# Attention beside a gated dense block on one core: three exponential patterns of a score tile, two of them summed by accumulating transfers

## The chip, the core and the metric

The kernel runs on one core of a Trainium2 chip. A core has a matrix engine (TensorE, PE in the profile), a vector engine (VectorE, DVE), a scalar engine (ScalarE, ACT), GpSimd (POOL) and SyncE (SP), which share an on-chip memory (SBUF). TensorE writes to a small accumulator memory (PSUM) that VectorE and ScalarE read. Transfers (DMAs) are issued from an engine's queue and run beside the engines; semaphores order all of it. The metric is the time of one execution on the device, in microseconds (us).

## The reference

The input `x` has 2048 rows of 512. All is bfloat16 at the ends.

```python
xn = _layernorm(x, axis=-1)
# A: 32 query heads of 16 on one shared key and value head
q = (xn @ wq) in 32 heads of 16;  k = xn @ wk;  v = xn @ wv
scores = einsum("bhqd,bkd->bhqk", q, k) * 16 ** -0.5
o = softmax(scores) @ v
s = o in one row of 512 @ wo
# B: dense 512 -> 1792 -> 512
g = silu(silu(xn @ w1) @ w2)
return x + s * g
```

## The kernel before, in words

**Tiles.** The queries are cut into four chunks of 512 and the heads into eight groups of four, so there are 32 groups of chunk and heads. A group has 16 key tiles of 128. A *tile* is a pair of group and key tile and has four *blocks*, one for each head: 128 keys by 512 queries. That makes 2048 blocks. A score matmul uses 32 rows of TensorE's array, so the four heads lie beside each other ("row" mode); the matmuls of the probabilities with V, and all dense ones, use 32 columns each, and four run beside each other ("col" mode). The planner calls four such a slot and gives a change of mode a price of its own.

**Two ways of taking an exponential.** A block goes to ScalarE or to VectorE.

- ScalarE (`exp_A`, line 576): TensorE puts two blocks into one of two PSUM pairs (`psA`, `fill_A`), and one instruction over 1024 columns writes both to `pa_sb`, a ring of 11. Each block is then owed one matmul with V (`emit_PV`, line 698).
- VectorE (`exp_D`, line 614): TensorE puts a block into one of three banks, `D`, `D1` or `F` (`fill_D`). VectorE adds a bias and writes the number as a 16-bit integer, whose bits read as bfloat16 are a piecewise linear power of two: a *pattern*. When the four blocks of a tile are there, GpSimd adds a constant to the integers (`shift`, line 639, as 64-bit words) and does so twice, which gives a second and a third pattern, shifted in phase. All three go into the sum with V, each with a weight of its own, so V is held four times (`vaug_sb`: once for ScalarE's blocks and once for each pattern). Such a tile is owed three matmuls with V for each block. A tile's patterns are held in one of four places (`ph_sb` three, `x_sb` one).

The last column of V's tile is the weight itself, so the same matmuls give the softmax's sum. When all that a group is owed has been added in `psO`, VectorE transposes it (`gn1`, line 769), takes the reciprocal (`gn2`), multiplies (`gn3`, line 786) and, for two groups, transposes back (`gn4`).

**Dense work.** The jobs `q` (queries), `h` (the first dense layer, 14 tiles of 512 for each chunk, into `u_sb`, two sets of 14), `z` (the second dense layer), `w` and `wp` (the product with `wo`) run on TensorE in bank `F`, between the scores (line 338). An `h` or a `z` is followed by a tanh on ScalarE (line 1014), 72 in all, and by a VectorE step (line 1046). A finished `w` goes through line 1058 into `fin_sb`, then an addition (line 1025) into `ob_sb`, and from there to the output.

**The order.** The queues of all engines are written out when the kernel is built. A class (`Sched`) holds a cost model of each engine and gives every instruction a due time; a loop emits, again and again, work for TensorE in col mode as long as ScalarE's next burst is not yet due, then a burst of scores for ScalarE (`score_run`) with blocks for VectorE riding in the rows that are free (`fill_D`); VectorE's steps are chosen by `advance_v`. A plan that does not come true on the chip is not mended there: each engine follows its written order and waits on semaphores.

Of the kernel before, what the change touches and what calls it, by code (L numbers as in the profile page):

```python
# [22 lines left out]
PH_SHIFT = (0, 43, 85)  # L23
PH_W = (0.2265625, 0.1787109375, 0.1416015625)
PH_ONE = 127 * 128
PH_BIAS = 65
NPH = len(PH_SHIFT)
LN2 = 0.6931471805599453
# [7 lines left out]
class Sched:  # L36
# [5 lines left out]
    def __init__(self):  # L42
        self.queues = {}
        self.done = {}
        self.clock = {}
        self.snap = {}
        self.last_w = {}
        self.readers = {}
        self.flagged = {}
        self.lanes = {}  # L50
        self.at = {}
        self.free = dict(pe=1.2, a=1.7, v=0.85, gp=0.7, sp=0.7)
        self.act_end = 0.0
        self.act_ends = []
        self.pe_mode, self.pe_last, self.pe_len, self.pe_tiles = None, 1.0, 0.0, set()
        self.pe_runs = []

# [37 lines left out]
    def model(self, eng, lane, cost, r):  # L95
        if lane:
# [27 lines left out]
        self.free[eng] = t + (cost or 0.4)  # L124
        return self.free[eng] + self.SEM
# [71 lines left out]
def bass_recurrent_scan__grouped_kv_mqa__dense_activation_silu__prompt_kernel(  # L197
# [25 lines left out]
    NPD = 4  # L223
    NPS = 3
    NGN = 2
    NOB = 4
    NWARM = 15
    NWARM2 = 0
    NWARM3 = 2
    NFRONT = 12  # L230
# [6 lines left out]
    NPAIR, LEAD_PAIR = 1, 1  # L237
    NF, F_FROM, F_LEFT, F_LATE, DENSE_END, HOLD, F_BEHIND = 14, 0.05, 9, 3, 0.97, 10, 0

    with ExitStack() as es:  # L240
# [15 lines left out]
        vaug_sb = sb("vaug_sb", [P, 1 + NPH, NKT, 32])  # L256
        qT_sb = sb("qT_sb", [P, 2, NDC, NQ])
        pa_sb = sb("pa_sb", [P, NPA, 2 * NQ])
        ph_sb = [sb(f"ph{j}_sb", [P, NPS, 4 * NQ], I16) for j in range(NPH)]
# [3 lines left out]
        u_sb = sb("u_sb", [P, 2, NFT, NQ])  # L263
        t_sb = sb("t_sb", [P, 2, NQ])
        tmp_sb = sb("tmp_sb", [P, 2, 4, D])
        fin_sb = sb("fin_sb", [P, 2, D])
# [6 lines left out]
        eps_sb = sb("eps_sb", [P, 1], FP32)  # L273
        mhalf_sb = sb("mhalf_sb", [P, 4], FP32)
        phw_sb = sb("phw_sb", [P, 1 + NPH], FP32)
# [37 lines left out]
        for j in range(NPH + 1):  # L313
            w = 1.0 if j == 0 else PH_W[j - 1]
# [40 lines left out]

        def aggr(t):
            op("v", lambda e: e.bn_aggr(mv_sb[:, t, :], stats_sb[:, t, :]), reads=[("st", t)], writes=[("mv", t)], cost=0.155)

        def rstd_pow(c):
            sl = slice(4 * c, 4 * c + 4)  # L360
            op("gp", lambda e: e.tensor_scalar(rstd_sb[:, sl], mv_sb[:, sl, 1], LN_EPS, None, op0=ALU.add),
               reads=[("mv", t) for t in tiles(c)], writes=[("rstd", c)])
            op("gp", lambda e: e.tensor_tensor(rstd_sb[:, sl], rstd_sb[:, sl], mhalf_sb[:, :], ALU.pow),  # L363
               reads=[("rstd", c), "mhalf"], writes=[("rstd", c)])
# [83 lines left out]
        def evac_V(c, bank, key):  # L448
            sh = [P, 1 + NPH, 4, DH]
# [26 lines left out]
        for t in tiles(0):  # L476
            stats(t)
        for t in tiles(0):
            aggr(t)
# [121 lines left out]
        def ph_ap(j, sl, a, b):  # L601
            if sl < 3:
                return ph_sb[j][:, sl, a:b]
            return x_sb[:, 4 * j:4 * j + 4, :].rearrange("p a b -> p (a b)").bitcast(I16)[:, a:b]

        def ph_key(j, sl, p):
            return ("ph", j, sl, p) if sl < 3 else ("x", 4 * j + p)

        def exp_D(blks):
# [8 lines left out]
            for b in blks:  # L618
                p = b["pos"]
                owe(tile[0], b["i"], tile[1], 1, ph_ap(0, sl, 512 * p, 512 * p + 512).bitcast(BF16), ph_key(0, sl, p), K.at[d])  # L620
# [8 lines left out]
        shifts = []  # L629

        def shift(tile, idx):
            sl, n = slot_of[idx], len(rows_of[idx])
            for j in range(1, NPH):
                if n < 4:
                    d = op("v", lambda e, j=j: e.tensor_scalar(ph_ap(j, sl, 0, NQ * n), ph_ap(0, sl, 0, NQ * n), float(PH_SHIFT[j]), None,
                                                               op0=ALU.add),
                           reads=[ph_key(0, sl, p) for p in range(n)], writes=[ph_key(j, sl, p) for p in range(n)], cost=0.4)
                else:
                    d = op("gp", lambda e, j=j: e.int64_add(ph_ap(j, sl, 0, 4 * NQ).bitcast(I64), ph_ap(0, sl, 0, 4 * NQ).bitcast(I64),  # L639
                                                            PH_SHIFT[j] * 0x0001000100010001),  # L640
                           reads=[ph_key(0, sl, p) for p in range(4)], writes=[ph_key(j, sl, p) for p in range(4)], cost=1.03)
                for p, i in rows_of[idx].items():
                    owe(tile[0], i, tile[1], 1 + j, ph_ap(j, sl, 512 * p, 512 * p + 512).bitcast(BF16), ph_key(j, sl, p), K.at[d])

        def may_D(blks):
            sl = slot_of[blks[0]["idx"]]
            return not any(held(ph_key(j, sl, p)) for j in range(1, NPH) for p in range(4)) and \
                not any(held(ph_key(0, sl, b["pos"])) for b in blks)
# [8 lines left out]
        def emit_PV(t, cap):  # L657
# [7 lines left out]
            while n < cap:  # L665
                cand = sorted((p for p in pend[gi] if p["at"] <= t + 0.216 * n and vready(p["kt"] // 4, t)), key=lambda p: p["at"])
# [28 lines left out]
                def f(e, st=st, cs=cs):  # L695
                    for p, s0, s1 in st:
                        i = p["i"]
                        r = e.matmul(psO[32 * i:32 * i + 32, cs], lhsT=vaug_sb[:, p["v"], p["kt"], :], rhs=p["ap"],  # L698
# [16 lines left out]
        def plan_D(gi, rows):  # L715
            owed[gi] += len(rows) * (NPH - 1)
            for i in rows:
                planned[gi][i] += NPH - 1
# [47 lines left out]
        def gn1(tk):  # L766
# [4 lines left out]
            task("gn2", gn2, 0.25, gi=gi, reads=[("otr", sl)], writes=[("rcp", sl)])  # L771
# [9 lines left out]
        def gn3(tk):  # L781
# [5 lines left out]
               reads=tk["reads"], writes=tk["writes"], cost=tk["cost"])  # L787
# [39 lines left out]

        dense = [("h", 0, ft) for ft in range(NFT)]
        for c in range(1, NC):
            for ft in range(NFT):  # L830
                dense.append(("h", c, ft))
                if ft in (2, 6, 9, 13):
                    dense.append(("z", 4 * (c - 1) + (2, 6, 9, 13).index(ft)))
# [32 lines left out]
        def startable(jb, t):  # L866
# [4 lines left out]
            if k == "h":  # L871
                return all(("zmm", 4 * (jb[1] - 2) + n) in tok for n in range(4) if jb[1] > 1) and K.ready("pe", ["w1"]) <= t + 0.1
# [548 lines left out]
```

## Time and profile before

| | |
|---|---|
| time, median of 3 runs | 676.95 us (676.89 to 676.99) |
| the profiled execution | 676.97 us |
| its span | 675.0 us |
| busy: TensorE, VectorE, ScalarE, GpSimd | 651.4, 588.9, 663.9, 369.1 us |
| exponentials on ScalarE (two blocks each) | 676 |
| blocks on VectorE | 696 |
| 64-bit additions on GpSimd (two for each tile of VectorE) | 348 |
| granted TensorE clock | 0.999 |

In the lines below, a group reads: line, engine, operation, written tile `<-` read tiles, shapes, count, then busy time in us and mean ns of one, then the engine's idle time just before such instructions and what ended it. In the chain and the timeline the first two numbers are the start and the length in us. Busy time on TensorE counts pipelined matmuls, so it can be high without the array being at its peak.

### The profile page before, as it was taken

How to read it: one execution, taken by the hardware profiler on the slowest of the kernel's cores; microseconds unless marked ns; L12 is line 12 of the kernel's file. 1: busy time of each engine (PE TensorE's matmuls, PEld its weight loads, DVE VectorE, ACT ScalarE, POOL GpSimd, SP SyncE). 2: the span in 40 equal slices, each digit the busy share in tenths (PEclk: the TensorE clock that was granted, in tenths of full speed). 3: DMA queues.
4: the chain of work that ended last, by engine and by line, in shares of the span. 5: the costliest groups of instructions: out<-in, count | busy, mean ns of one | idle time of the engine just before them, and what ended most of it. 6: DMA issues, size and time to landing. Idle time of an engine off the chain costs nothing.

```text
span 675.0 us, 18633 instructions
## 1 busy us (share of the span) xinstructions
PE 651.4 (96%) x8167; PEld 184.3 (27%) x8174; DVE 588.9 (87%) x1005; ACT 663.9 (98%) x762; POOL 369.1 (55%) x373
## 2 busy tenths in 40 slices
PE   8999999999999999999999999999999999999997
PEld 4422222222222222222222222222222222222221
DVE  7898788888798979999898988899898988888996
ACT  6999999999999999999999999999999999999997
POOL 3155455564555646565564655566564646654653
PEclk9999999999999999999999999999999999999999
DMA  6340000000000001000000000010000000000110
GB/s 178 134 146 2 1 2 1 2 2 1 2 1 2 2 17 34 18 1 2 2 1 2 1 2 2 1 33 18 17 2 2 2 2 1 2 2 1 34 33 32
DMA packets 12337, 12.50 MB, mean 19 GB/s; under 512 B 2528, under 2 KB 11744, under 8 KB 12256
## 3 DMA queue, kind: packets, MB, share of 16 engines
q1 hardware_dynamic: 11680, 10.78, 5.2%
q8 instruction: 64, 1.05, 0.7%
q10 hardware_dynamic: 576, 0.52, 0.2%
q14 instruction: 17, 0.14, 0.1%
HBM read 8.95 MB, written 2.10 MB: 16 GB/s over the span
## 4 chain that ended last, share of the span: by engine, by line
ACT 78%; PE 14%; DVE 3%; issue 1%; POOL 1%; DMA 1%; SPq 0%; POOLq 0%
ACT pa_sb L576 73%; PE psA L546 5%; ACT t_sb L1014 5%; PE psO L698 4%; PE psF L338 4%; DVE ph_sb L614 1%; DMA x_sb<-in_A_x_dram 1%; DVE stats_sb L354 1%; POOL ph_sb L639 1%; POOL rstd_sb L363 0%; DVE xn_sb L375 0%; PE psD L546 0%; PE psD L386 0%; PE psD L417 0%; DVE kTa_sb L429 0%
## 5 line engine op out<-in xcount | busy, mean ns | idle before, releaser
L576 ACT ACTIVATE pa_sb<-psA 128x1024 bf16<-128x1024 f32 x676 | 642.9, 1198 | 1.9 <-PE psA L546 1.7
L639 POOL INT64_ADD ph_sb<-ph_sb x290 | 300.7, 1049 | 221.8 <-DVE ph_sb L614 221.8
L614 DVE TENSOR_SCALAR ph_sb<-psD 128x512 int16<-128x512 f32 x527 | 351.8, 682 | 54.7 <-PE psD L546 47.9
L698 PE MATMUL psO<-ph_sb,vaug_sb 128*32 128x512 bf16 x1740 | 215.6, 383 | 0.2
L698 PE MATMUL psO<-pa_sb,vaug_sb 128*32 128x512 bf16 x1360 | 206.2, 383 | 0.4 <-ACT pa_sb L576 0.4
L546 PE MATMUL psA<-qT_sb,kTa_sb 32*128 32x512 bf16 x692 | 134.2, 385 | 6.8 <-ACT pa_sb L576 5.0
L546 PE MATMUL psA<-qT_sb,kTb_sb 32*128 32x512 bf16 x652 | 126.4, 384 | 7.9 <-ACT pa_sb L576 7.0
L546 PE MATMUL psD<-qT_sb,kTb_sb 32*128 32x512 bf16 x330 | 118.4, 384 | 0.4 <-DVE ph_sb L614 0.4
L546 PE MATMUL psD<-qT_sb,kTa_sb 32*128 32x512 bf16 x307 | 111.7, 384 | 0.1
L639 POOL INT64_ADD x_sb<-x_sb x58 | 60.2, 1050 | 49.7 <-DVE x_sb L614 49.7
L614 DVE TENSOR_SCALAR x_sb<-psD 128x512 int16<-128x512 f32 x110 | 74.2, 680 | 10.5 <-PE psD L546 9.1
L546 PEld LDWEIGHTS psA<-qT_sb,kTa_sb 32*128 32x128 bf16 x692 | 32.4, 91 | 148.2 <-ACT pa_sb L576 136.0
L338 PE MATMUL psF<-xnT_sb,w_sb 128*32 128x512 bf16 x896 | 70.4, 384 | 0.0
L546 PEld LDWEIGHTS psA<-qT_sb,kTb_sb 32*128 32x128 bf16 x652 | 30.6, 91 | 144.1 <-ACT pa_sb L576 136.6
L338 PE MATMUL psF<-w_sb,u_sb 128*32 128x512 bf16 x896 | 69.0, 384 | 0.0
L698 PEld LDWEIGHTS psO<-ph_sb,vaug_sb 128*32 128x32 bf16 x1740 | 53.4, 95 | 50.4 <-issue 33.8
L698 PEld LDWEIGHTS psO<-pa_sb,vaug_sb 128*32 128x32 bf16 x1360 | 50.6, 94 | 44.1 <-issue 33.2
L698 PE MATMUL psO<-x_sb,vaug_sb 128*32 128x512 bf16 x348 | 60.9, 384 | 0.0
L1014 ACT ACTIVATE t_sb<-psF 128x512 bf16<-128x512 f32 x72 | 56.6, 786 | 0.0
L1046 DVE SCALAR_TENSOR_TENSOR u_sb<-t_sb,psF 128x512 bf16<-128x512 bf16 x56 | 38.3, 683 | 6.1 <-ACT t_sb L1014 5.0
L614 DVE TENSOR_SCALAR ph_sb<-psF 128x512 int16<-128x512 f32 x53 | 35.9, 678 | 0.0
L546 PEld LDWEIGHTS psD<-qT_sb,kTb_sb 32*128 32x128 bf16 x330 | 28.2, 91 | 0.8 <-issue 0.7
(124 smaller groups left out, 351.6 us busy)
## 6 DMA issues: line engine op xcount, KB each, us to landing
w_sb<-in_B_w_dram SPq DMA_DIRECT2D x2, 1792.0 KB, 8.7
x_sb<-in_A_x_dram SPq DMA_DIRECT2D x18, 128.0 KB, 2.2
out_dram<-ob_sb SPq DMA_DIRECT2D x14, 128.0 KB, 1.7
x_sb<-in_A_x_dram SPq DMA_DIRECT2D x3, 512.0 KB, 7.1
wop_sb<-in_A_wo_dram SPq DMA_DIRECT2D x1, 512.0 KB, 5.6
wq_sb<-in_A_wq_dram SPq DMA_DIRECT2D x1, 384.0 KB, 6.7
x_sb<-in_A_x_dram ACTq DMA_DIRECT2D x2, 128.0 KB, 2.9
kTb_sb<-kTa_sb SPq DMA_DIRECT2D x16, 16.0 KB, 1.8
```

The source lines that it names most:

```text
L338: r = e.matmul(bank[32 * i:32 * i + 32, :], lhsT=lhsT[:, 32 * i:32 * i + 32], rhs=rhs, start=start, stop=stop, tile_position=(0, 32 * i), ...
L354: op("v", lambda e: e.bn_stats(stats_sb[:, t, :], x_sb[:, t, :]), reads=[("x", t)], writes=[("st", t)], cost=0.687)
L546: return e.matmul(ap, lhsT=kT_sb[g % 2][32 * i:32 * i + 32, kt * P:(kt + 1) * P], rhs=qT_sb[32 * i:32 * i + 32, c % 2, g // 2, :], start=T ...
L576: d = op("a", lambda e: e.activation(pa_sb[:, sl, :], psA[k][:, :], ACT.Exp, scale=ESCALE), reads=["A%d" % k], writes=[("pa", sl)], cost=2 ...
L614: d = op("v", lambda e: e.tensor_scalar(ph_ap(0, sl, 512 * pos, 512 * pos + m), src, float(PH_ONE + PH_BIAS), 0.0, op0=ALU.add, op1=ALU.ma ...
L639: d = op("gp", lambda e, j=j: e.int64_add(ph_ap(j, sl, 0, 4 * NQ).bitcast(I64), ph_ap(0, sl, 0, 4 * NQ).bitcast(I64), PH_SHIFT[j] * 0x0001 ...
L698: r = e.matmul(psO[32 * i:32 * i + 32, cs], lhsT=vaug_sb[:, p["v"], p["kt"], :], rhs=p["ap"], start=s0, stop=s1, tile_position=(0, 32 * i) ...
L1014: op("a", lambda e: e.activation(t_sb[:, n % 2, :], bank_ap(b), ACT.Tanh, scale=0.5 if jb[0] == "h" else 0.25), reads=[b], writes=[("t", n ...
L1046: op("v", lambda e: e.scalar_tensor_tensor(out=dst, in0=t_sb[:, n % 2, :], scalar=1.0, in1=src, op0=ALU.add, op1=ALU.mult), reads=tk["read ...
```

## The change

- A tile of VectorE after the front has two matmuls with V for each block. GpSimd adds the constant for the second pattern as before, then issues a transfer that adds the first pattern, as bfloat16, to the second in place (`accum_op`). The sum is one operand. When the transfer has landed, the third pattern is written over the first (`flush_later`) and is the other operand. Tiles of the front, and those of the last group that begin late, keep three operands. The planner gives such a transfer 4.7 us to land (`SUM_LAND`), and GpSimd's issue 0.92.
- The patterns lie in seven places of a pair each (eleven buffers in `ph_sb`, three in `x_sb`). V is held in three weights instead of four.
- `u_sb` is a ring of 23 tiles; the four `z` jobs of a chunk stand after the third, fifth, seventh and ninth `h` of the next chunk, before after the third, seventh, tenth and fourteenth. `fin_sb` goes; line 1058's result is written to `ob_sb` and the addition is done there in place.
- After ScalarE's burst, `extra_fill` can add blocks for VectorE in a further burst, in a bank that comes free within 0.3 us, where by the plan VectorE gains more than 0.25 us by it. Other new options of the planner (`row_want`, `TWIN`, `JOINT`, `FRESH`) are off in this rule set; `LEAD` goes from 3 to 4 and the dense jobs begin 16 tiles in instead of 12.
- The planner models waits between GpSimd and VectorE's instructions with two inputs in SBUF, and delays `gn3` and the addition of a row (`DEFER`, `PATIENCE`) until GpSimd's present work is planned to end.
- In the front, one of the first four tiles' statistics is taken on ScalarE by two passes with accumulated sums; 13 instead of 15 warm-up matmuls. At the end, two rows that ScalarE stored one by one go in one transfer.

```diff
-PH_SHIFT = (0, 43, 85)
-PH_W = (0.2265625, 0.1787109375, 0.1416015625)
+PH_SHIFT = (0, 42, 88)
+PH_W = (1.0, 0.1953125, 0.1416015625)
+PH_OF = (0, 1, 1, 2)
+SUM_LAND = 4.7
...
-    NPD = 4
-    NPS = 3
+    SUML_END, DEFER, PATIENCE = 9, 0.2, 8
+    SUML, VGAIN = 6, 9
+    NPD = 7
+    NPB = 11
+    NU = 23
...
+        A=(0.2, 3.0, 0.65, 10, 1.2, 2.0, 0, 12, 0.2, 4, 3, 0.0, 0.25, 0.43, 0, 0.33, 0, 0, 5, 9, 0.3, 7),
...
+            (SLIP, ROUND, KEEP, HOLD, AGES["gn1"], AGE, F_BEHIND, ENDQ, PVWAIT, LEAD, AHEAD, MARGIN, XGAIN, AIM, TWIN,
+             TGATE, FRESH, JOINT, SUML, VGAIN, XWAIT, XHOLD) = \
+                RULES[PLAN[min(int(K.act_end / STRETCH), len(PLAN) - 1)]]
...
+            flush_later(K.ready("gp", first, other_))
+            d = op("gp", lambda e: e.int64_add(whole(1, sl), whole(0, sl), PH_SHIFT[1] * 0x0001000100010001),
+                   reads=first, writes=other_, cost=1.03)
+            if idx in summed:
+                d = op("gp", lambda e: e.dma_start(whole(1, sl, dt=BF16), whole(0, sl, dt=BF16), accum_op=ALU.add),
+                       reads=first, writes=other_, lane=f"sum{sl}")
+            owe_D(tile, idx, 1, 2, K.at[d])
...
+            later.append(dict(tile=tile, idx=idx, sl=sl, at=K.at[d] if idx in summed else None))
...
+        def flush_later(t):
+            for x in list(later):
...
+                if x["at"] > t + 0.1 if x["at"] is not None else any(held(k) for k in first):
+                    continue
...
+                    d = op("gp", lambda e, sl=sl: e.int64_add(whole(0, sl), whole(0, sl), PH_SHIFT[2] * 0x0001000100010001),
+                           reads=first, writes=first, cost=1.03)
+                owe_D(x["tile"], x["idx"], 0, 3, K.at[d])
...
+        def extra_fill():
+            t = K.pe_last + K.pe_len
+            if sum(held(("pa", k)) for k in range(NPA)) >= XHOLD or group_A() >= NGRP or (XOPEN and jst["open"]) or (XBEH < 99 and behind(XBEH)):
+                return
+            advance_v(t + 0.05)
...
+            for b in BANKS:
+                if hold[b] is None and (b != "F" or not jobs or not behind(F_BEHIND) or not next_job(t)):
+                    r = max(t, K.ready("pe", [], [b]))
+                    gain = max(vfree, ride) - max(vfree, r + 0.43)
+                    if r <= t + XWAIT and gain > XGAIN + XCOST * (r - t):
...
+            fill_D(best[0], [0, 1, 2, 3], [best[1]])
...
+                        if not front and len(rows) == 4 and (new[0] > group_A() or len(left[new[0]]) >= (SUML_END if new[0] == NGRP - 1 else SUML)):
+                            summed.add(dst["idx"])
+                        plan_D(new[0], rows, NPH - (dst["idx"] in summed))
...
+        Z_AT = (2, 4, 6, 8)
+        def on_u(c, ft):
+            return (NFT * c + ft) % NU
...
-        for t in tiles(0):
+        stats_act(1)
+        for t in (0, 2, 3):
             stats(t)
...
-        store(0, "a")
         copy(1, ob_sb[:, 1, :], ("ob", 1), bank_ap("D1"), "D1")
-        store(1, "a")
+        op("a", lambda e: e.dma_start(ov[:, t0:t0 + 2, :], ob_sb[:, 0:2, :]), reads=[("ob", 0), ("ob", 1)],
+           writes=[("out", t0), ("out", t0 + 1)], lane="st01a")
```

274 lines of the change are left out of this document (204 added, 70 removed).

## The prediction

> **What bounds the kernel now.** I read the page's first two parts, then the groups, then the wait lists of the vector engine's line, then one stretch of the timeline.
>
> ```profile
> span 675.0 us, 18633 instructions
> PE 651.4 (96%) x8167; PEld 184.3 (27%) x8174; DVE 588.9 (87%) x1005; ACT 663.9 (98%) x762; POOL 369.1 (55%) x373
> ...
> L576 ACT ACTIVATE pa_sb<-psA 128x1024 bf16<-128x1024 f32 x676 | 642.9, 1198 | 1.9 <-PE psA L546 1.7
> L639 POOL INT64_ADD ph_sb<-ph_sb x290 | 300.7, 1049 | 221.8 <-DVE ph_sb L614 221.8
> L614 DVE TENSOR_SCALAR ph_sb<-psD 128x512 int16<-128x512 f32 x527 | 351.8, 682 | 54.7 <-PE psD L546 47.9
> ```
>
> ScalarE is full: it idles 1.9 us before 676 exponentials. The chain of waits shows their spacing:
>
> ```profile
> 56.85 5.50 ACT pa_sb L576 x6
> 62.84 3.67 ACT pa_sb L576 x4
> 67.00 3.67 ACT pa_sb L576 x4
> ```
>
> Four take 3.67 us, 0.917 each (1198 ns overlap), and a tanh in between adds 0.49 (62.84 + 3.67 to 67.00). So 676 x 0.917 = 620, 72 tanh x 0.49 = 35, 10.5 before the first exponential, 7.2 after the last, 1.9 idle: 675. The time falls when ScalarE gets fewer blocks. An exponential does two blocks (0.459 us each); the other 696 of the 2048 go to VectorE's line 614. So the question is why VectorE, with 86 us idle, takes no more.
>
> ```profile
> L614 DVE TENSOR_SCALAR ph_sb<-psD x527: 626/684/693, 26.3 to 660.1; 128x512 int16<-128x512 f32 x176
> ...
>   PE psD L546: 57.0, 203
>   PE psF L546: 2.8, 14
> ```
>
> 59.8 us of it, in 217 waits, is VectorE waiting for TensorE to fill a score bank. The mean is 0.28 us; counted one by one in the trace, 69 of them are over 0.25 and make 31.1 us. TensorE, over one round:
>
> ```profile
> 302.63 0.61 PE L338 MATMUL psF<-xnT_sb,wq_sb 128*32 128x512 bf16 x8
> 303.18 0.39 PE L546 MATMUL psA<-qT_sb,kTb_sb 32*128 32x512 bf16 x2
> 303.19 0.39 PE L546 MATMUL psD<-qT_sb,kTa_sb 32*128 32x512 bf16 x1
> 303.50 0.62 PE L338 MATMUL psF<-xnT_sb,wq_sb 128*32 128x512 bf16 x8
> 304.07 0.39 PE L546 MATMUL psA<-qT_sb,kTb_sb 32*128 32x512 bf16 x2
> ```
>
> A score burst leads to the next work 0.32 later (303.18 to 303.50) and two slots of four matmuls lead to the next burst 0.57 later. That is 0.89 of ScalarE's 0.917. A slot is 0.22 (0.61 for eight against 0.39 for four). A third slot would be late, so TensorE is full in whole slots, and VectorE gets its block when ScalarE's burst comes round, no earlier.
>
> **The change, part by part.** The balance first. A block on VectorE costs 466.0/696 = 0.67 us of busy time (line 614 over all tiles: 351.8 + 74.2 + 35.9 + 4.1) and takes 0.459 off the span. An idle microsecond of VectorE that becomes work is 1/(0.67 + 0.459) = 0.89 block, or 0.41 us of span.
>
> *Summing.* The 174 tiles of four blocks (348 adds / 2) give three patterns each, so three slots; line 698 shows 1740 + 348 of these matmuls, 522 slots. A summed tile gives two. All are summed but those begun in the front (before about 34 us, where the first add stands) and the last group's late ones: I take 170. That frees 170 x 0.22 = 37 us of TensorE.
>
> *The extra burst* (`extra_fill`) spends it. It stands right behind ScalarE's burst, in the same mode, so it costs one slot and no change of mode, and takes a bank that comes free up to 0.3 us later, where VectorE gains over 0.25 us. Bounds: only the 69 long waits go, 31.1 us, or -12.6; all 217 go, 59.8 us, or -24.3. I take the row that pays for it, 170 freed slots against 217 waits: 0.78 x 59.8 = 46.8 us, **-19.0** (41 blocks, ten tiles more, 184 in all).
>
> *GpSimd* per tile: an add (1.05), the issue of the transfer, an add (1.05). No row shows such an issue: 0.34 is SyncE's for a store, 1.05 a whole add; I take 1.05, as GpSimd's own instruction is nearest. 184 x 3.15 = 580 of some 660 us, 88% against 55%. It stays off the path while a tile takes under 3.59 (660/184), a margin of 0.44. Cost 0 to the point in the second rival.
>
> *The locks.* VectorE's additions with two SBUF inputs meet GpSimd:
>
> ```profile
> L786 DVE TENSOR_TENSOR onb_sb<-otr_sb,rcp_sb x31: 406/411/1207, 45.1 to 654.2; 128x256 bf16<-128x256 f32 x31
> ```
>
> Median 411, longest 1207; the group's mean of 520 makes 0.11 us lost at 55% of GpSimd. There are 43 (31, and 12 at line 1025). With more of GpSimd and with the planner's new delay of these steps, I take 0.2 us more each: 8.6 us of VectorE, **+3.5**. Bounds: none, and 0.8 each (1207 - 411): +14. The Trainium skill, SBUF — State Buffer, section "Who interferes with whom", says that a VectorE instruction with two SBUF inputs contends with a GpSimd instruction that reads SBUF and that the second to issue fully blocks; the 1207 against 1.05 for an add agrees. By that rule alone, a random meeting at 88% costs half an add, an estimate of 0.46 us each and +8, so the sum would be 665.
>
> *The transfer.* Rows: 16 KB inside SBUF land in 1.8 us, 512 KB from HBM in 5.6.
>
> ```profile
> kTb_sb<-kTa_sb SPq DMA_DIRECT2D x16, 16.0 KB, 1.8
> ...
> wop_sb<-in_A_wo_dram SPq DMA_DIRECT2D x1, 512.0 KB, 5.6
> ```
>
> The planner in the diff assumes 4.7 (`SUM_LAND`). This one is 512 KB inside SBUF with the destination read too; between the rows I take the planner's value, at no cost. The Trainium skill, DMA: Bandwidth & Descriptors, section "Anatomy of one DMA", gives 2.0 us plus the bytes over 436 GB/s: an estimate of 3.2 us, or 4.4 with the destination's bytes counted as well, under the plan's 4.7 either way; no run here shows it.
>
> *The new wait.* The second add stands in GpSimd's order and waits for the landing; queued behind it are the next tile's first add and its issue, and TensorE's pattern matmuls wait for those. A summed pattern is ready some 6.8 us after the last block (1.05 + 1.05 + 4.7), the third at 7.9, against 1.05 and 2.1 now. A tile must be begun with five of ScalarE's left (`LEAD` 4), 9.2 us; four blocks at 0.9 and 7.9 make 11.5. The 2.3 left over are covered by ScalarE's ring of 11 (ten microseconds). Gone, that cover costs up to 2.3 a group, 74 us over 32; I take 0.
>
> *Front and end.* One of four statistics moves to ScalarE, which is idle for 2.94 us before line 368. VectorE does 0.6 less there, ScalarE two passes of 0.6 behind a load landing at about 3.6 (0.73 + 2.9), ready near 5.1 against 5.83: **-0.5** (bounds -0.7 to +1.3, a table load of 1.28). In the end the second copy no longer waits 0.48 behind a store's issue, and the last store leaves so much sooner: **-0.4** (0 if the double store lands later).
>
> *With one answer:* the ring of 23 dense tiles and the earlier second jobs (TensorE's order within the slots; four must be done before the tenth of the next chunk), the dropped `fin_sb` (line 1058's result waits for a store of four rows before, 1.7 us, rows tens of microseconds apart), one weight of V fewer, 13 warm-up matmuls: 0 each, as ScalarE's 0.917 hides them; a dense job held up for a whole round costs one slot.
>
> **Sum** against the profiled execution's 676.97 (span 675.0 and 1.97 around it; the median is 676.95, so nothing to correct): -19.0 + 3.5 - 0.5 - 0.4 = -16.4, **660.5 us**. A measurement of this kernel tells 0.2%, 1.35 us, from no change.
>
> **Rivals.**
> 1. *The rounding stays.* The 148 waits under 0.25 come from ScalarE's rhythm and stay, since the extra burst asks for a gain over 0.25. For it: the spacing of bursts. Against: freed slots also let a burst come when a bank is free. -12.6 + 3.5 - 0.9: 667.
> 2. *The transfer lands late (slower).* Place: the second add of line 639. The margin is 0.44 a tile, and the gain of 16.4 over 184 tiles 0.09, so from a landing 0.53 after the plan, 5.2 us, the kernel is slower. At wop's 5.6, a delay of 0.9 less 0.44 is 0.46 a tile, 85 us if every tile pays, 42 if every second does: 660.5 + 42, about 703. For it: that row; the order is fixed when the kernel is built. Against: no HBM in it, and seven places.
> 3. *The locks bite*: 0.46 to 0.8 each, +8 to +14: 665 to 671, 669. For: 1207. Against: median 411, and the delay. The skill's rule above is this rival.
> 4. *All waits close*: -24.3 - 0.9 with no more locks: 652. The 7.3 us before lines 1046's results may go too: 649.
> 5. *The change does not do what it says*: no place of pairs is free when a tile is wanted, and the plan makes as many tiles as before: 676.
>
> **Chances.** Forecast (655 to 666) 0.46; rival 1 0.13; rival 3 0.10; rival 4 0.14; rival 2 0.13; rival 5 0.04. Faster 0.83, same 0.04, slower 0.13. The range goes from 645 (rival 4, with a little over) to 682, which leaves out most of rival 2.
>
> **What would show it.** Right: about 655 exponentials at line 576 and some 184 tiles on GpSimd (368 adds, about as many issues as tiles less the front's); line 698's pattern matmuls near 1500; line 614's idle time for psD near 15 us; GpSimd near 85 to 90%; line 786's mean under 720 ns. Wrong: GpSimd idle before its adds until a DMA, landings over 5.2 us, TensorE waiting for GpSimd, ScalarE idle by more than a few microseconds, or as many exponentials as now.

## The result, and the profile after

The changed kernel takes **696.83 us** (691.71 to 707.75, three runs), 1.0255 times the kernel before, interval [1.0235, 1.0275]. The forecast was 660.5 with a range to 682; it was wrong, and on the wrong side. The ratio leaves out the longest of the three, which ran in a slow state of the chip (707.75 us, granted clock 0.955 against 0.979 and 0.982). That execution was also the profiled one, so the lines below are of a later profiled execution of the same kernel: 693.94 us, span 692.1, clock 0.983.

The page of the changed kernel. Line 610 is now the scores, 640 ScalarE's exponential, 687 VectorE's, 734 GpSimd's first add, 737 the issue of the accumulating transfer, 762 the second add, 819 the matmuls with V.

```profile
span 692.1 us, 17428 instructions
PE 655.3 (95%) x7489; PEld 186.8 (27%) x7492; DVE 606.6 (88%) x992; ACT 662.7 (96%) x759; POOL 520.7 (75%) x540
...
L640 ACT ACTIVATE pa_sb<-psA 128x1024 bf16<-128x1024 f32 x667 | 633.4, 1126 | 19.4 <-PE psD L610 11.6
L687 DVE TENSOR_SCALAR ph_sb<-psD 128x512 int16<-128x512 f32 (+1 forms) x645 | 435.7, 706 | 64.7 <-PE psD L610 61.8
L762 POOL INT64_ADD ph_sb<-ph_sb x170 | 203.2, 1209 | 55.2 <-DMA ph_sb<-ph_sb 45.1
```

Three things are to be seen. The change does what it says: pattern matmuls with V fall from 2088 to 1498, and 161 tiles are summed. But exponentials fall only from 676 to 667, so ScalarE lost 9 x 0.917 = 8.3 us of work where I had counted on 19. And ScalarE, which was never short of work, now idles 19.4 us before its exponentials. A new wait is the largest of GpSimd's: 45.1 us before the second add, for the transfer. With the other tiles' places it is 52.6 us in 56 waits.

The plan that the kernel is built with (its own cost model's end of ScalarE's last instruction) ends at 672.1 us for the kernel before, and the chip's span was 675.0. For the changed kernel it ends at 663.3, and the span was 692.1. So the change is planned to win 8.8 us, and 29 are lost between plan and chip, against 3 before. The experiments ask where.

The timeline of the changed kernel shows how the first of them go:

```profile
36.49 1.17 POOL L737 DMA_DIRECT2D ph_sb<-ph_sb  x1 [0.32 <-POOL ph_sb L734]
...
46.30 0.40 PE L819 MATMUL psO<-ph_sb,vaug_sb 128*32 128x512 bf16 x4 [2.37 <-DMA ph_sb<-ph_sb]
46.36 1.03 POOL L762 INT64_ADD ph_sb<-ph_sb  x1 [6.12 <-DMA ph_sb<-ph_sb]
47.07 2.12 ACT L640 ACTIVATE pa_sb<-psA 128x1024 bf16<-128x1024 f32 x2 [2.26 <-PE psD L610]
...
51.62 1.02 ACT L640 ACTIVATE pa_sb<-psA 128x1024 bf16<-128x1024 f32 x1 [0.48 <-PE psD L610]
```

The transfer issued at 36.49 lands at 46.3, 9.8 us later; the loads of `wop_sb` and of the dense weights were issued at 34.1 and 34.8 and move beside it. TensorE stands 2.37 us in front of the summed pattern, GpSimd 6.12 in front of its second add, and ScalarE 2.26 for scores that TensorE could not start. Then comes an afterglow: exponentials 1.4 us apart, each with 0.48 of idle time, while TensorE's granted clock is 0.62 (46 to 52 us). At 334 us, after a stop of TensorE of 2.02, the trace shows pairs of score matmuls of 0.61 us that take 0.39 otherwise.

### The profile page after: what moved, and what is told of

Its sections match the earlier page's. It is cut to its first block, busy times and chain, and to the rows that moved or that the text cites. A ratio compares the mean times of both kernels' runs of the same rounds, so it can differ in the third digit from the quotient of the medians.

```text
span 705.9 us, 17428 instructions
## 1 busy us (share of the span) xinstructions
PE 671.3 (95%) x7489; PEld 186.7 (26%) x7492; DVE 605.2 (86%) x992; ACT 663.7 (94%) x759; POOL 520.9 (74%) x540
## 4 chain that ended last, share of the span: by engine, by line
ACT 47%; PE 27%; DVE 12%; POOL 7%; DMA 6%; issue 2%; SPq 0%
ACT pa_sb L640 44%; PE psA L610 9%; PE psF L389 7%; PE psO L819 7%; DVE ph_sb L687 6%; DMA ph_sb<-ph_sb 6%; ACT t_sb L1142 3%; POOL ph_sb L762 2%; POOL ph_sb L734 2%; PE psD L610 2%; POOL ph_sb L737 1%; DVE onb_sb L908 1%; DVE ob_sb L1153 1%; POOL x_sb L734 1%; PE psO L389 1%
## 5 line engine op out<-in xcount | busy, mean ns | idle before, releaser
L687 DVE TENSOR_SCALAR ph_sb<-psD 128x512 int16<-128x512 f32 (+1 forms) x645 | 436.5, 706 | 79.8 <-PE psD L610 76.7
L762 POOL INT64_ADD ph_sb<-ph_sb x170 | 204.8, 1226 | 50.0 <-DMA ph_sb<-ph_sb 39.8
L734 POOL INT64_ADD ph_sb<-ph_sb x152 | 176.2, 1159 | 36.8 <-DVE ph_sb L687 36.4
L819 PE MATMUL psO<-ph_sb,vaug_sb 128*32 128x512 bf16 x1360 | 161.0, 392 | 6.1 <-DMA ph_sb<-ph_sb 5.3
L819 PE MATMUL psO<-pa_sb,vaug_sb 128*32 128x512 bf16 x1342 | 163.8, 390 | 2.9 <-DMA ph_sb<-ph_sb 1.4
L737 POOL DMA_DIRECT2D ph_sb<-ph_sb x137 | 120.1, 877 | 42.5 <-POOL ph_sb L734 41.3
L610 PE MATMUL psD<-qT_sb,kTb_sb 32*128 32x512 bf16 x348 | 129.2, 403 | 3.8 <-DVE ph_sb L687 3.2
L819 PEld LDWEIGHTS psO<-pa_sb,vaug_sb 128*32 128x32 bf16 x1342 | 41.0, 95 | 52.2 <-issue 36.9
L819 PEld LDWEIGHTS psO<-ph_sb,vaug_sb 128*32 128x32 bf16 x1360 | 40.1, 95 | 51.1 <-issue 29.2
L610 PEld LDWEIGHTS psD<-qT_sb,kTa_sb 32*128 32x128 bf16 x351 | 27.9, 91 | 13.3 <-DVE ph_sb L687 11.8
L734 POOL INT64_ADD x_sb<-ph_sb x20 | 22.5, 1123 | 7.7 <-DVE ph_sb L687 7.7
```

Of the source, the lines that this page charges most:

```text
L610: return e.matmul(ap, lhsT=kT_sb[g % 2][32 * i:32 * i + 32, kt * P:(kt + 1) * P], rhs=qT_sb[32 * i:32 * i + 32, c % 2, g // 2, :], start=T ...
L687: d = op("v", lambda e: e.tensor_scalar(ph_ap(0, sl, 512 * pos, 512 * pos + m), src, float(PH_ONE + PH_BIAS), 0.0, op0=ALU.add, op1=ALU.ma ...
L734: d = op("gp", lambda e: e.int64_add(whole(1, sl), whole(0, sl), PH_SHIFT[1] * 0x0001000100010001), reads=first, writes=other_, cost=1.03)
L737: d = op("gp", lambda e: e.dma_start(whole(1, sl, dt=BF16), whole(0, sl, dt=BF16), accum_op=ALU.add), reads=first, writes=other_, lane=f"s ...
L762: d = op("gp", lambda e, sl=sl: e.int64_add(whole(0, sl), whole(0, sl), PH_SHIFT[2] * 0x0001000100010001), reads=first, writes=first, cost ...
L819: r = e.matmul(psO[32 * i:32 * i + 32, cs], lhsT=vaug_sb[:, PH_OF[p["v"]], p["kt"], :], rhs=p["ap"], start=s0, stop=s1, tile_position=(0, ...
```

## The experiments

All times stand beside runs of the kernel before on the same chip (medians of 676.99 to 677.05 us). "Plan" is where the kernel's own written order ends; spans, waits and lines are of the one profiled execution of each kernel.

**1. Is it the same again?** The changed kernel, unedited.

> The changed kernel once more, for a second trace. If the stalls are a matter of the written order: late by the same steps at the same places (47, 99, 167, 303 and 346 us). If they are chance (landings differ from run to run): other places but the first, and 690 to 708 us.

695.9 us, 1.0279 [1.0244, 1.0313]. The stops lie at the same places of the order as in the first trace (47, 98, 161, 291 to 304 and 335 us); only their sizes differ.

**2. Is it the summing?** Two kernels: nothing is summed (three patterns each, all else as changed), and the transfer copies instead of adding, in the same order.

```diff
-                            summed.add(dst["idx"])
+                            pass
```

> The changed kernel with no tile summed: three patterns for each block as before the change, no transfer; the extra burst, the seven places, the ring and all else stay. The plan ends 12 us after the changed kernel's (680 exponentials, so fewer blocks on VectorE than the kernel before). Theory A and B: no late landing, no half clock, 679 to 683 us, 0.3 to 0.9% slower than the kernel before and faster than the changed one. Theory C: with GpSimd at half load the locks go too, the same number, so this run tells A and B from C only by line 908's mean (under 550 ns in all). If the stalls come from the extra burst or the ring: 690 or more.

679.75 us, 1.0048 [1.0033, 1.0064], on a plan of 675.4 with 680 exponentials; ScalarE idles 1.2 us:

```profile
L640 ACT ACTIVATE pa_sb<-psA 128x1024 bf16<-128x1024 f32 x680 | 645.0, 1200 | 1.2 <-PE psA L610 0.9
```

So the loss comes with the summing, and all other parts together cost 2.8 us.

```diff
-  ... e.dma_start(whole(1, sl, dt=BF16), whole(0, sl, dt=BF16), accum_op=ALU.add),
+  ... e.dma_start(whole(1, sl, dt=BF16), whole(0, sl, dt=BF16)),
```

> The changed kernel, in the same written order, with the transfer copying the first pattern over the second instead of adding it: the sum is left out of the computation, all instructions and waits stay. If adding in the transfer is what takes 4.9 us to land: under 4.2, GpSimd's waits for landings near 0, and the time at its plan, 668 to 674. If it is the 512 KB alone, or the queue: landing 4.5 to 5 as now and 688 to 708.

679.7 us, 1.0037 [1.0024, 1.0051]. The lists of transfers (count, KB, median us from issue to landing), first of the changed kernel, then of this one:

```profile
ph_sb<-ph_sb POOLq DMA_DIRECT2D x137, 512.0 KB, 4.9
```

```profile
ph_sb<-ph_sb POOLq DMA_DIRECT2D x137, 512.0 KB, 2.9
```

The same order with a landing of 2.9 us instead of 4.9 (and an issue of 0.55 instead of 0.87) is 16 us faster. In the changed kernel no transfer lands in less than 4.49, the plan has 4.7, and 48 of 161 take over 5.2. GpSimd's waits for landings fall from 52.6 to 8.8 us. The time is above the 668 to 674 that I expected: the span still stands 14.6 us above the plan of 663.3 that it shares with the changed kernel. Set against the due times of that plan, the changed kernel is 24.0 us late at its last exponential and this one 7.4; another 5.1 us pass after the last store has landed (see "Front and end" below).

**3. Does the plan lack room for the landing, or does the clock carry the loss?** Three kernels: summing only after the planner's 52nd us; that, and 6.5 us for a landing in the plan instead of 4.7; and, for the clock, filler matmuls in every free slot (`KEEP` 0.65 to 1.1).

```diff
-  if not front and len(rows) == 4 and (...
+  if not front and K.act_end > 52 and len(rows) == 4 and (...
-SUM_LAND = 4.7
+SUM_LAND = 6.5
```

> The changed kernel, with no tile summed before the planner's 52 us, so that the first transfers (landing 9.96 us) no longer run beside the loads of the dense weights. The plan ends 2.8 us later. Theory A and B: the first of the five stalls, 6.4 us of lateness in the profile, goes and the other four stay: 688 to 704 us. If the other stalls follow from the first one: 672 to 680. Theory C: 693 to 710.

686.4 us, 1.0142 [1.0106, 1.0177]: without the stop at 47 us, 10 us less, a little under the forecast. Stops remain, but not at the old places: the longest are now at 250 and 632 us.

> As the one that sums nothing before 52 us, and the planner gives a transfer 6.5 us to land instead of 4.7, so that GpSimd's second add and TensorE's matmuls of the sum come later in the written order. The plan ends 5 us later than the changed kernel's (672 exponentials). Theory A and B: GpSimd's waits for landings go from 40 us to a few, no stretch at half clock is left, ScalarE idles under 5 us, 672 to 677 us. Theory C: VectorE's two-input steps and GpSimd's adds take as long as before, 695 to 712.

677.61 us, 1.0012 [1.0, 1.0024], a little over the forecast. From its page:

```profile
L640 ACT ACTIVATE pa_sb<-psA 128x1024 bf16<-128x1024 f32 x672 | 638.2, 1176 | 2.4 <-PE psA L610 2.1
...
L762 POOL INT64_ADD ph_sb<-ph_sb x163 | 209.9, 1313 | 7.8 <-PE psO L819 3.7
```

The landings are as before (median 4.92, 42 over 5.2), but of line 762's idle time the largest part is now for TensorE, with 3.7 us in 4 waits left for landings on all its tiles, and ScalarE idles 2.4. The loss against the plan falls from 29 to 5.9 us (this was the shortest of ten executions; at the median it is 7.5). Against `e_late` one number alone differs, `SUM_LAND`, and the time falls by 8.8 us. It was the order's missing room, not the transfers' work.

> The changed kernel with one number of the planner changed: filler matmuls are put into every free slot of TensorE (the threshold of activity goes from 0.65 to 1.1), some 130 matmuls more. Its plan ends 0.2 us later than that of the changed kernel. Theory A (a late transfer only starts the loss; most of it is TensorE at half clock for some 10 us after it has been idle for 1 to 2 us): with the free slots filled the stretches at half clock become fewer or shorter, granted clock over 0.985, 676 to 688 us. Theory B (the late transfers themselves cost the time, the clock only follows): unchanged within the kernel's own spread, 690 to 708. Theory C (locks between GpSimd and VectorE): unchanged, 690 to 708.

694.55 us, 1.0296 [1.0234, 1.0357], at a clock of 0.974 to 0.991, against 0.972 to 0.983 in `a_again`. With the clock somewhat better kept the time is the same, and the landing waits are too (52.5 us). That speaks for the waits themselves; how much the lowered clock behind each stop adds is not separated.

**4. Had the kernel before that room?** It gets extra instructions on GpSimd ahead of its 40th, 80th and 120th tile, without a place in its plan: first 2, 4 and 6 of another kind, then 14, 28 and 42 small adds.

```diff
+            for _ in range({40: 14, 80: 28, 120: 42}.get(len(calls), 0)):
+                op("gp", lambda e: e.int64_add(scr_i..., scr_i..., 1), ..., cost=1e-6)
```

> The kernel before, with three delays that its plan does not know: ahead of the additions of the 40th, 80th and 120th tile GpSimd does 2, 4 and 6 small instructions of 1.04 us (2.1, 4.2 and 6.2 us), nothing else. It measures what a late operand costs without any transfer. Theory A (half clock after an idle TensorE makes a stall dearer than itself): the delays that reach TensorE for over a microsecond are followed by some 10 us at a granted clock under 0.8 and cost 5 to 7 us each, 10 to 20 us in all, 687 to 697. Theory B (only the wait itself): each costs at most its length less the slack of some 2 us, 0 + 2 + 4, no dip of the clock, 680 to 684.

719.19 us, 1.0624. A miss: ScalarE stopped 11.4, 8.2 and 16.5 us, far more than the instructions' own 2 to 6: GpSimd stood 7.0 us before the first instruction of the other kind (1.04 us each) and 6.0 to 6.2 before its next add, with nothing to wait for in the profile. GpSimd was thus some 15, 17 and 19 us late.

> The kernel before, with three delays that its plan does not know, now of the same kind of instruction that GpSimd runs there anyway: 14, 28 and 42 small 64-bit additions (0.18 us each by the row of the one at line 512, so 2.5, 5 and 7.5 us or less if they overlap) ahead of the additions of the 40th, 80th and 120th tile. Theory A: each that reaches TensorE costs its wait and, at half clock, several exponentials at 1.4 us instead of 0.92, together 3 us or more on top of the wait, granted clock under 0.99; 684 to 695. Theory B: the waits alone, 680 to 686.

689.1 us, 1.0178 [1.0158, 1.0199]. The delays measured 3.90, 8.07 and 12.19 us. The first two stopped ScalarE nowhere. After the third:

```profile
486.87 1.02 ACT L576 ACTIVATE pa_sb<-psA 128x1024 bf16<-128x1024 f32 x1 [9.21 <-PE psD L546]
```

So the kernel before took a GpSimd that was 3.9 and 8.1 us late for nothing at two places. The room differs by place: of the 12.19 us only some 3 were covered, and of `b_stall`'s three delays some 4, 9 and 3. In the changed kernel the stop at 335 us follows a landing of 6.01 us, 1.3 over the plan. That patterns queue up before a full TensorE, and that this queue went with its fullness, is my reading and not shown; nor was the changed kernel given the same delays.

**5. What is the extra burst worth?** The kernel of `e_land` with it off (`XGAIN` 9).

> As the kernel that plans 6.5 us for a landing and sums nothing before 52 us, with the extra burst off. Its plan ends 9 us after that one's (676 exponentials instead of 672, more idle time of ScalarE in the plan). Theory A and B: no stall, the time at its plan, 681 to 686 us, so the extra burst is worth 5 to 8 us and summing alone gains nothing. If the freed slots alone feed VectorE as my prediction's rival had it: 668 to 677.

693.9 us, 1.0242 [1.0225, 1.0259], 676 exponentials, plan 677.3: 16 us slower than with it, 9.0 of that planned, and above both forecasts. The rest is lateness: line 908's step took 2.59 us at 194 us and ScalarE stopped at 199, and again at 244 and 248. So 9 us is what the plan gives for the burst; what it is worth in an order that keeps its plan was not measured.

**6. What is left: VectorE's two-input steps?** `e_best65` has a landing of 6.5 us and rule A's parameters set for a shorter plan (663.3 us; `KEEP` 1.1, `LEAD` 5, `AIM` 0.5, `XWAIT` 0.45); `e_best70` a landing of 7.0 (plan 664.9).

> As the kernel that plans 6.5 us for a landing and sums nothing before 52 us, with five numbers of the planner set for a better plan: fillers in every free slot, LEAD 5, an extra burst that may wait 0.45 us for a bank, and an aim of 0.5. Its plan ends 5 us earlier (666 exponentials). Theory A and B: 670 to 674 us, faster than both kernels. Theory C (locks): no better than 677.

678.6 us, 1.002 [0.9995, 1.0046]; landing waits 2.4 us. It came out as the theory of the locks had it: the landings hardly wait, and the time is no better.

> As the kernel with a planned landing of 6.5 us and the better plan, but a planned landing of 7.0, LEAD 6, an extra burst that may wait 0.3 us and wants a gain of 0.4. Its plan ends 1.7 us later (668 exponentials) and leaves more room. If room for the landing decides: 672 to 676 us, faster than both kernels. If the locks decide: 675 to 680, no better.

686.96 us, 1.0151 [1.012, 1.0182]; landing waits 0.8, but line 908 has a mean of 1033 ns against a shortest of 407. This order, with more room for the landing, ended above both forecasts.

Then `e_best65` with line 908 as a reciprocal of one input, and with a product by 1.0.

```diff
-  e.tensor_tensor(d3, o3, rcp_sb[:, sl, :]..., ALU.mult),
+  e.reciprocal(d3, o3)                                  # e_nolock
+  e.tensor_scalar(d3, o3, 1.0, None, op0=ALU.mult),     # e_nolock2
```

> As the kernel with a landing of 6.5 us and the better plan (666 exponentials, 678.6 us), but line 908 has one input instead of two: it writes reciprocals of the transposed sums instead of the sums times the reciprocal, so the normalisation is left out of the computation; the order is the same. Theory C for what is left of the loss (a two-input step of VectorE held for 2 to 3.4 us by GpSimd makes the next score burst late): line 908's longest falls under 0.7 us, ScalarE idles under 3 us, 668 to 672 us. If the rest comes from the transfers or the clock alone: 674 to 680 as now.

709.34 us, a miss of its own: a reciprocal takes 1.74 us, not 0.41.

```profile
L910 DVE RECIPROCAL onb_sb<-otr_sb 128x256 bf16<-128x256 f32 x31 | 54.0, 1742 | 0.1
```

It shows two things, though. The 31 steps took 54.0 us, where line 908 took 23.8 in `e_best65`, its waits included: 30 us more of VectorE, unplanned, cost 31 us, about one a microsecond. And none of the 31 waited: the shortest took 1.735 us and the longest 1.753, though GpSimd was at work beside 30 of them.

> The kernel of e_best65 (planned at 663.3 us, measured at 678.6) with one further edit: the step that normalises the first attention output multiplies by the constant 1.0 instead of by the reciprocal of the row sums (the normalisation is left out), so it reads one SBUF tensor instead of two. Its mean in e_best65 was 766 ns with a largest of 3397 ns. Theory (what keeps e_best65 15 us above its plan is VectorE's two-input steps that wait beside GpSimd's adds, each 1 to 3 us late, with no queue left at ScalarE): the step's largest time stays under 0.7 us, the 1 to 2 us idle stretches of ScalarE behind such steps go, and the time is 668 to 672 us. Rival (the residue is landings and the clock, the steps only happen to lie near): the steps become short and the time stays at 676 to 680 us.

674.84 us, 0.9964 [0.9953, 0.9976]: better by 3.8, not by the 7 or more expected, and the step still took up to 2.79 us. Its timeline shows why:

```profile
469.72 3.38 POOL L762 INT64_ADD ph_sb<-ph_sb  x3
...
470.94 2.31 DVE L908 TENSOR_SCALAR onb_sb<-otr_sb 128x256 bf16<-128x256 f32 x1
...
474.77 0.38 PE L610 MATMUL psD<-qT_sb,kTa_sb 32*128 32x512 bf16 x1 [1.42 <-DVE ph_sb L687]
...
476.07 1.02 ACT L640 ACTIVATE pa_sb<-psA 128x1024 bf16<-128x1024 f32 x1 [1.60 <-PE psD L610]
```

Behind a transfer's issue at 469.11, three adds of GpSimd run back to back to 473.10, and VectorE's step, begun at 470.94 and 0.28 long in the median, ends at 473.25. So this step with one input waits as well, where the reciprocal did not. VectorE's blocks are then 2 us late, TensorE stands in front of a score bank, and ScalarE stops. The Trainium skill, SBUF — State Buffer, section "Who interferes with whom", names `tensor_scalar` too among what can contend with GpSimd; the 2.31 agrees. Until 440 us this kernel was on its plan; it lost 1.5 us at 443, behind line 1153's step of 1.97, 3 here and 3 at 577, behind an issue, two adds and a step of 2.79.

**7. Which engine needs the room?** TensorE takes a tile of patterns only 1.5 us after its planned readiness, the landing staying at 4.7 (`e_late_m15`, against `e_late`), and room at both places (`e_slack`: also landing 5.2 and a milder rule A).

```diff
-  p["at"] <= t + 0.216 * n and ...
+  p["at"] + (p["v"] > 0) * 1.5 <= t + 0.216 * n and ...
```

> The kernel of e_late (planned at 666.1 us, measured at 686.4) with one edit in the planner: TensorE takes a tile of patterns only 1.5 us after the moment at which the planner holds it ready, the landing in the plan staying at 4.7 us and GpSimd's order being planned as before. Its plan ends at 666.8 us. Theory (the loss is made at TensorE, which stands behind a late tile in its written order, and 1.5 us of room there covers most landings): GpSimd still waits for landings some 35 to 45 us in all, ScalarE idles under 6 us, and the time is 673 to 679 us. Rival (GpSimd's own wait, which pushes all its later tiles, carries the loss): as e_late, 684 to 688 us.

689.5 us, 1.0211 [1.0167, 1.0255]. No help: GpSimd waits 57.2 us for landings, its later tiles slip behind the plan steadily (by 1 us at 174, by 17 at 668), and TensorE's room is used up. That GpSimd's own wait carries the loss fits this, but it is argued: by its last exponential ScalarE is 14.7 us late too.

> Summing only after the planner's 52nd us, the landing in the plan raised from 4.7 to 5.2 us, TensorE taking a tile of patterns 1.5 us after its planned readiness, and milder parameters for filling and for the second burst of exponentials; its plan ends at 667.3 us. Theory (room at both places, for GpSimd and for TensorE, is what the changed kernel lacks): waits of GpSimd for landings under 25 us, ScalarE idle under 5 us, 671 to 676 us, which would be below the kernel before. Rival (VectorE's locked steps take any room, as in the two kernels with the larger landing): 677 to 684 us.

680.87 us, 1.0059 [1.0028, 1.009], as the rival had it; landing waits 22.4, but VectorE's steps wait 21.1.

**8. Other orders of the same work.** Three plans with the same parts, summing from 60 or 75 us on, landings planned at 6.25 or 6.5, other parameters. `e_r3`, against the changed kernel:

```diff
-SUM_LAND = 4.7
+SUM_LAND = 6.5
-        A=(0.2, 3.0, 0.65, ..., 0.2, 4, 3, 0.0, 0.25, 0.43, ..., 0.3, 7),
+        A=(0.1, 3.0, 1.1, ..., 0.2, 4, 3, 0.0, 0.3, 0.5, ..., 0.4, 7),
-  if not front and len(rows) == 4 and (...
+  if not front and K.act_end > 75 and len(rows) == 4 and (...
```

> Summing only after the planner's 60th us, the landing in the plan at 6.25 us, TensorE taking a tile of patterns 0.4 us after its planned readiness, more fillers, and rule A's parameters for the second burst changed; its plan ends at 662.3 us. It was picked among some hundred such plans as one whose order is disturbed least when the landings vary as in the traces (4.5 to 7 us) and a two-input step of VectorE has to wait for GpSimd's running adds. Theory (the loss of the changed kernel is lateness in a written order, by landings and by those waits, and an order that has room where they fall keeps its plan): waits of GpSimd for landings under 12 us, ScalarE idle under 8 us, 670 to 674 us, below the kernel before. Rival (each order meets such waits somewhere, and a plan of about 663 us always ends 12 us or more above itself): 675 to 682 us.

671.97 us, 0.9923 [0.9908, 0.9937]: as forecast, with landing waits of 5.5 us and ScalarE idle for 2.7.

> As e_r1 with other parameters: summing after the 75th us, landing 6.25 us, TensorE's room 0.8 us, fewer fillers; its plan ends at 664.1 us. Theory: 671 to 675 us, ScalarE idle under 8 us. Rival: 676 to 683 us.

681.14 us, 1.0064 [1.0048, 1.0081]: as the rival had it, with landing waits of 0.7 us and lock waits (see below) of 18.2.

> As e_r1 with other parameters: summing after the 75th us, landing 6.5 us, no room of TensorE beyond that, as many fillers; its plan ends at 662.5 us. Theory: 671 to 675 us, ScalarE idle under 8 us. Rival: 676 to 683 us.

**668.77 us**, 0.9878 [0.9863, 0.9892], below both kernels. Its page, and its line 908 (shortest/median/longest ns):

```profile
span 666.2 us, 17828 instructions
PE 651.8 (98%) x7686; PEld 185.1 (28%) x7686; DVE 596.5 (90%) x1007; ACT 657.3 (99%) x758; POOL 520.5 (78%) x536
...
L640 ACT ACTIVATE pa_sb<-psA 128x1024 bf16<-128x1024 f32 x666 | 632.0, 1165 | 1.4 <-PE psA L610 0.6
...
L762 POOL INT64_ADD ph_sb<-ph_sb x164 | 209.2, 1303 | 4.6 <-PE psO L819 3.1
```

```profile
L908 DVE TENSOR_TENSOR onb_sb<-otr_sb,rcp_sb x31: 408/416/1627, 44.5 to 650.2; 128x256 bf16<-128x256 f32 x31
```

The work is that of the changed kernel within a few tiles: 666 exponentials against 667, 155 summed tiles against 161, 358 adds against 356. The landings are no better (median 5.0, 50 of 155 over 5.2). But GpSimd waits 1.0 us for them against 52.6, ScalarE idles 1.4 against 19.4, and the span stands 3.7 us above its plan against 28.8. Ten exponentials fewer than before at 0.917 are 9.2 us; the span fell by 8.8. Of three orders picked with one aim, though, one ended in its forecast, one 6 us above it and this one 2 below: how much of it is the order's room and how much luck in where the waits fall, three runs do not tell.

Across the kernels, with what line 908's and line 1153's steps took over their undisturbed time summed up as "lock waits" (us, to some 0.3, by what is taken as undisturbed):

| kernel | plan | span - plan | landing waits | lock waits |
|---|---|---|---|---|
| before | 672.1 | 2.9 | 0 | 3.6 |
| e_nosum | 675.4 | 2.3 | 0 | 4.8 |
| e_r3 | 662.5 | 3.7 | 1.0 | 6.2 |
| e_land | 668.3 | 5.9 | 3.7 | 11.6 |
| e_nolock2 | 663.3 | 9.8 | 1.1 | 12.3 |
| e_r1 | 662.3 | 7.8 | 5.5 | 12.6 |
| e_best65 | 663.3 | 12.2 | 2.4 | 14.9 |
| e_r2 | 664.1 | 15.2 | 0.7 | 18.2 |
| e_best70 | 664.9 | 19.6 | 0.8 | 24.5 |
| e_copy | 663.3 | 14.6 | 8.8 | 11.0 |
| e_land_noextra | 677.3 | 15.2 | 9.1 | 14.8 |
| e_slack | 667.3 | 14.7 | 22.4 | 21.1 |
| e_late | 666.1 | 16.8 | 48.6 | 7.4 |
| e_late_m15 | 666.8 | 20.9 | 57.2 | 14.4 |
| changed | 663.3 | 28.8 | 52.6 | 15.4 |
| e_keep | 663.5 | 29.1 | 52.5 | 14.5 |

Where landings hardly wait (the first nine), the loss goes with the lock waits, at (2.9 + ... + 19.6) / (3.6 + ... + 24.5) = 79.4/108.7 = 0.73 us each. The last four lie far above that line: 7.4 would make 5 and was 17, 15.4 would make 11 and was 29. The three rows between fit it less well: `e_slack` is on it, `e_copy` and `e_land_noextra` are 7 and 4 us above. So in the changed kernel some 11 us go with the locks and some 17 with the landings and the lowered clock behind them. This split is an estimate from the table, and a correlation. The landings' part has a second witness in `e_copy`, 24.0 - 7.4 = 16.6 us less lateness at the last exponential in the same order; the locks' part has none, as no run took them away alone.

Why there are more lock waits than before can be read from the traces. Over all twenty of them, take the steps of line 908 or 1153 (786 or 1025 before) that came more than 0.1 us late out of a run of GpSimd's instructions. Where the run was of adds alone, one right behind the other, the step waited for the running add only (48 of 48; 0.79 us for a step of 0.41 in the kernel before). Where the run held the issue of a transfer, the step waited until all of it was over (64 of 67). Runs of the second kind came with the change; without transfers (`e_nosum`) the lock waits are 4.8 us.

## Why the prediction was wrong

- **What bounds the kernel** was right: the time follows the number of exponentials at 0.917 us as long as ScalarE has work (`e_r3`: 9.2 reckoned, 8.8 measured). What I did not ask is how much lateness the order can take. The "86 us idle" and the waits for banks told of VectorE; nothing in my reading told how late a pattern may be.
- **The failed step: "I take the planner's value, at no cost", and "covered by ScalarE's ring of 11 ... I take 0".** 4.7 us is nearly the shortest landing (4.49), not the middle (median 4.9, mean 5.1, longest 9.8). I even named what is queued behind the waiting add, and then covered it with a ring that holds ScalarE's results; what was needed is scores for ScalarE, which a TensorE standing in front of a late pattern cannot make (2.37 us of TensorE and 2.26 of ScalarE at 47 us). The rival of the late landing, at 703, was right in place (the second add), side and size (696.8), and I gave it 0.13. Its price was off in form: not a GpSimd past its limit (it was 75% busy, not the 88% I reckoned), but lateness in a written order. By the rival's own threshold of 5.2 us the median landing of 4.9 would have cost nothing, so that its size came near is luck.
- **The skill's figure for the transfer.** The Trainium skill, DMA: Bandwidth & Descriptors, section "Anatomy of one DMA", gave an estimate of 3.2 or 4.4 us. The copy measured 2.9, a little under the first; the accumulating transfer is above the second at its best, 4.49.
- **The extra burst (-19.0) was over-sized.** Foreseen were 41 more blocks, there are 18 (20 in `e_r3`), -8.3 to -9.2. "170 freed slots against 217 waits" was no measure: VectorE's waits for banks went from 59.8 us to 64.5 in the changed kernel and to 42.3 in `e_r3`, where 17.5 us closed and not 46.8. Even the lower bound, 31.1 us or -12.6, was too much. Part of the freed slots stayed without work: `e_r3` fills 69 with idle matmuls, 25 more than the kernel before. With nothing late, nine exponentials fewer would have made 676.97 - 8.3 = 669 (an estimate).
- **The locks (+3.5) were near as VectorE time, wrong as price.** I added 8.6 us to 3.9; measured were 15.4. But 0.41 us of span for one of VectorE holds for an average microsecond, while these come 1 to 2 us at once on an order without room, at 0.73 by the table (`e_nolock` had about one).
- **GpSimd's tile** took 1.04 + 0.30 + 0.87 + 1.04, 3.25 us (the second add begins 0.3 before the issue's record ends and is longer by as much), against 3.15: right, and not the limit.
- **Front and end**: the -0.5 is not shown. The Sqrt of the statistics came 0.3 us earlier in the first trace (5.55 against 5.87) and 0.25 later in the second (6.12), where the first load landed at 3.86 instead of 3.27. At the end nothing was won: the span ends 2.5 to 2.9 us after the last store has landed, against 0.5 before. What ends last is GpSimd: it reaches the close of the program at 691.94, 5.4 us after its last instruction, and SyncE at 689.82; in `e_copy` 7.0 after. `e_r3` with 155 such transfers ends 0.5 after its last store, GpSimd 3.3 after its last instruction, so why is open.
- **The rest at 0**: without summing, all other parts together, the extra burst among them, cost 2.8 us, so they won nothing; no run takes the parts at 0 one by one.
- Of the signs named for a failure, GpSimd idle until the DMA, landings over 5.2 and ScalarE idle by more than a few microseconds all came.

## What to carry to other kernels

Where engines follow an order that is written out ahead, ask of every new wait not only what it costs on average but how late its release can be and what queue covers that; taking work off the full engine may take away the queue in front of it, and with it the room that hid lateness elsewhere (a reading; no run shows the queue). Plan with a time that most transfers meet (here 6.5 us, not 4.7): the changed kernel at 697 and the one at 669 us do nearly the same work with the same landings. That was needed but not enough: with 6.25 to 7.0 us planned, `e_best65`, `e_best70` and `e_r2` still ended 12 to 20 us above their plans. And compare the span with the plan, as the difference tells at once whether a loss was planned or came on the chip.

## What the runs showed of the hardware

- An accumulating transfer of 512 KB inside SBUF, issued from GpSimd, landed in 4.49 us at best, 4.9 in the median, and 9.8 beside the loads of the dense weights; a copy of the same bytes in 2.84 at best and 2.9 in the median. Its issue took 0.87 us of GpSimd against 0.55.
- A step of VectorE that meets GpSimd's adds waited for one of them where the adds ran alone (48 of 48 cases, 0.79 us for a step of 0.41), and nearly always for the whole run where a transfer's issue was part of it (64 of 67, 2.31 us for a step of 0.28). One input in SBUF was no protection for the product with a constant; the reciprocal never waited (1.735 to 1.753 us, 31 of 31).
- After a stop of 2 us TensorE's matmuls took 0.61 us instead of 0.39 for some microseconds (granted clock 0.62 from 46 to 52 us), and exponentials came 0.48 to 0.49 us late each.
- GpSimd stood 6.9 to 7.1 us when it changed from its adds to another kind of arithmetic, and 6.0 to 6.2 when it changed back (`b_stall`).
